# Attention and a four-expert layer on one core: second products only in runs of two token tiles

## The chip, the core and the metric

The kernel runs on one core of a Trainium2 chip. The metric is the device time of one execution in microseconds (us), the median of several runs; less is better.

## What is computed

The reference is block-sparse attention followed by a mixture of four experts, all in float32.

```python
# attention: batch 4, 8 heads, 768 tokens, head size 64, blocks of 32 tokens
scores = q @ k.T / 8
mask = |block_i - block_j| <= 1, or first/last block on either side, or one of 3 sampled blocks
attn = softmax(where(mask, scores, -1e9)); x = (attn @ v) as [3072 tokens, 512]
# experts: 512 -> 1024 -> 512, weighted by normalised probabilities p
for e in range(4):
    out += p[:, e:e+1] * (maximum(x @ w1[e], 0) @ w2[e])
```

## The kernel before

TensorE (PE in the rows) does nearly all of the work, on float32 values split into a high and a low part (`copy` to fp32r and a subtraction), so that one product is three matmuls.

The tokens come in five sets: batch 0 as two plain sets of 384 tokens, batches 1 to 3 as sets of 768. Each set runs through eight chunks of 512 hidden columns (four experts, two chunks each).

- A **first product** (`first`, L714) makes one piece of the hidden layer: six matmuls of 384 columns into one bank of PSUM, `w` or `v`. The plain sets take eight a chunk (`PLAIN`, two per hidden tile; L725 in the rows). The last three sets use a Strassen-like scheme with seven products of half size for eight; a chunk is two halves of `2, 1, 5, 6, 3, 7, 4` (`ORDER`, L628; L746). Products 2, 5 and 3 go to bank `v`, the others accumulate in bank `w`, which product 1 opens anew. Readers take intermediate sums out of the banks: ScalarE copies `v` after 2 (L767) and 5 (L773); VectorE adds out of `w` after 1 (L769), 6 (L776) and 7 (L781), and out of `v` after 3 (L778). A finished hidden tile gets ReLU on ScalarE (`hh`, L753; in the plain sets L734) and its low part on VectorE (`hl`, L754; L735). The last tile of a half is read straight out of `w`: after product 4, `hh` and then `hl` must be done before the next half's product 1 may write `w`.
- A **second product** (`second`, L787) multiplies one hidden tile (index f, 0 to 3) of one token tile (j, 0 to 2) with `w2`: three matmuls of 512 columns (L795) into one of three banks `po`, one for each token tile. After f = 3 VectorE adds the bank into the output rows `oacc` (L810); the next round may then write the bank.

Operands are made seven first products ahead (`operands`, `NWO`): ScalarE casts (L674), GpSimd subtracts (L675), and VectorE makes the sums of weights in place (L678 to L684; L682 overwrites what L675 read). `split_w2` (L692) does the same for `w2` (L698, L699).

Attention for the next batch (units `Group` and `Edge`) is fed in between: scores into two banks (`S`, L347 and L480), transposes into the same two banks (`T`, L385 and L502), weighted values (`A`, L416 and L531). Gathered rows come by GpSimd's DMA (L212). `attend` (L1008) places each part by a count of product time; the scores are placed only after a second product (`drive(..., 2)`). At the end of a batch `conversion` (L582) turns the attention output into the seven operands of the next set; VectorE does large subtractions there (L597, L594), starting eight first products before the set ends.

The order of products is fixed when the program is built, in `experts` (L827): `lead` gives each second product the count of first products after which it is due, ten or more after its tile was begun. A step yields either one second product, if due, or one first product. `hl` of a first product is recorded one step later (`defer`), behind whatever that step records on VectorE.

Of the kernel before, what the change touches and what calls it, by code (L numbers as in the profile page):

```python
# [23 lines left out]
def attention_moe_kernel(ctx: ExitStack, tc, qb, kb, vr, sampled, sampled_t, probs, w1, w2, out):  # L24
# [193 lines left out]
    one = const.tile([1, 1], F32, name="one")  # L218
# [8 lines left out]
    lead = p1.tile([NR, G], F32, name="lead")  # L227
# [392 lines left out]
    def convert(b, r):  # L620
        if b in todo and todo[b][0][0] <= r:
            step(b)

    def need(b, n):
        while b in todo and any(m == n for _, _, m in todo[b]):
            step(b)
# [5 lines left out]
    def plain(m):  # L632
        return m < 2
# [80 lines left out]
    def first(b, c, s, n):  # L714
        ps_m, cp, hp = later["m"], later["c"], later["h"]
        w = wo.pop((b, c, s, n))
        if plain(b):
# [10 lines left out]
            if k == 1:  # L728
                f = 2 * s + i
                ring = int((c * FT + f + FT) % (NH[0] + NH[1]) >= NH[0])  # L730
                hh = hp.tile([P, HS], F32R, name=f"hh{ring}", bufs=NH[ring])
                hl = hp.tile([P, HS], F32R, name=f"hl{ring}", bufs=NH[ring])
                src = W[s]
# [16 lines left out]
        def finish(half, g, src):  # L750
            hh = hp.tile([P, HS], F32R, name=f"hh{g}", bufs=NH[g])
            hl = hp.tile([P, HS], F32R, name=f"hl{g}", bufs=NH[g])
            nc.scalar.activation(hh, src, AF.Relu)  # L753
            defer.append(lambda: nc.vector.scalar_tensor_tensor(hl, src, 0.0, f32(hh), op0=ALU.max,  # L754
                                                                op1=ALU.subtract))
            hs[c, 2 * s + half, g] = (hh, hl)
# [65 lines left out]
    TB = NCH * (len(ORDER) * T1 + KT * FT * T2)  # L822
    TP = NCH * (len(PLAIN) * T1 + KT // 2 * FT * T2)
    OFF = 10
    NH = (5, 3)

    def experts():  # L827

        sets = []
        ends = [0]  # L830
        for b in range(SETS):
            sets.append(([(b, c, s, n) for c in range(NCH) for s, n in (PLAIN if plain(b) else ORDER)],
                         [(b, c, g, f, j) for c in range(NCH) for g in ((0,) if plain(b) else (1, 0))
                          for f in range(FT) for j in range(HS // P)]))
            ends.append(ends[-1] + len(sets[-1][0]))
        one = [x for a, _ in sets for x in a]
        two = [x for _, a in sets for x in a]

        lead = [ends[b] + i * len(a) / len(t) + OFF for b, (a, t) in enumerate(sets) for i in range(len(t))]

        def ready(p):

            q = 0
            for b, (a, t) in enumerate(sets):
                q += min(max(p - OFF + 1 - ends[b], 0), len(a)) * len(t) // len(a)
            return q

        p = q = 0
        after_first = False
        while q < len(two):  # L850

            left = defer[:]
            defer.clear()
            wait = after_first and p < len(one) and one[p][3] == 4 and q < ready(p)
            if wait or p >= min(len(one), lead[q]):
                second(*two[q])
                q += 1
                after_first = False
                took = T2, 2
            else:  # L860
                need(one[p][0], one[p][3])
                first(*one[p])
                p += 1
                after_first = True
                took = T1, 1
            for op in left:
                op()
            for b in todo:
                if p - ends[b] >= EARLY:
                    convert(b, p - ends[b])  # L870
                    break
            yield took

    stream = experts()
    done = [0.0]

# [238 lines left out]
```

## Time and profile before

| | us |
|---|---|
| median of 3 runs | 1249.38 (1248.95 to 1249.69) |
| profiled execution | 1256.33 |
| its span | 1254.6 |
| TensorE matmuls busy | 1228.3 |
| VectorE / ScalarE / GpSimd busy | 759.5 / 675.6 / 715.1 |

The profiled execution is one run, taken with the profiler on; its own time stands beside the span that the rows cover. Matmuls overlap, so the length of a row is longer than the time until the next one starts; the distance of two starts is what a piece costs TensorE. Some rows merge several matmuls.

### The profile page before, as it was taken

How to read it: one execution, taken by the hardware profiler on the slowest of the kernel's cores; microseconds unless marked ns; L12 is line 12 of the kernel's file. 1: busy time of each engine (PE TensorE's matmuls, PEld its weight loads, DVE VectorE, ACT ScalarE, POOL GpSimd, SP SyncE). 2: the span in 40 equal slices, each digit the busy share in tenths (PEclk: the TensorE clock that was granted, in tenths of full speed). 3: DMA queues.
4: the chain of work that ended last, by engine and by line, in shares of the span. 5: the costliest groups of instructions: out<-in, count | busy, mean ns of one | idle time of the engine just before them, and what ended most of it. 6: DMA issues, size and time to landing. Idle time of an engine off the chain costs nothing.

```text
span 1254.6 us, 29430 instructions
## 1 busy us (share of the span) xinstructions
PE 1228.3 (98%) x11028; PEld 1051.0 (84%) x11028; DVE 759.5 (61%) x1743; ACT 675.6 (54%) x1817; POOL 715.1 (57%) x846
## 2 busy tenths in 40 slices
PE   5899999999999999999999999999999999999998
PEld 3688888878888888888888888888888888888887
DVE  5455536545448676656658676666756855555553
ACT  4556645666656446666665445666664544444441
POOL 5566656666659646555546664556544855555551
PEclk9899999999999999999999999999999999999999
DMA  8556646585635425444413442444431222222211
GB/s 242 159 184 172 192 167 214 181 233 183 189 104 196 152 77 153 151 126 124 131 60 131 160 125 84 138 153 135 142 91 47 89 97 66 67 70 68 66 51 54
DMA packets 75051, 163.84 MB, mean 131 GB/s; under 512 B 8923, under 2 KB 20188, under 8 KB 74908
## 3 DMA queue, kind: packets, MB, share of 16 engines
q1 hardware_dynamic: 69238, 144.65, 36.8%
q0 software_dynamic: 5632, 17.31, 5.0%
q8 instruction: 87, 1.43, 0.5%
q14 instruction: 56, 0.46, 0.1%
q10 hardware_dynamic: 38, 0.00, 0.0%
HBM read 155.63 MB, written 6.29 MB: 129 GB/s over the span
## 4 chain that ended last, share of the span: by engine, by line
PE 67%; DVE 2%; issue 0%; POOL 0%; POOLq 0%; DVEq 0%
PE po L795 32%; PE w L746 16%; PE v L746 12%; PE s L347 2%; PE o L416 2%; PE tp L385 1%; DVE oacc L810 1%; PE ow L531 1%; PE sw L480 1%; PE tw L502 0%; DVE d L597 0%; DVE hl L754 0%; DVE r L682 0%; PE w L725 0%; PE v L725 0%
## 5 line engine op out<-in xcount | busy, mean ns | idle before, releaser
L675 POOL TENSOR_TENSOR wo<-r,wo 128x256 fp32r<-128x256 f32 x288 | 241.2, 840 | 278.5 <-ACT wo L674 275.0
L795 PE MATMUL po<-h,hh 128*128 128x512 f32 x768 | 307.4, 400 | 1.4 <-DVE oacc L810 1.4
L795 PE MATMUL po<-h,hl 128*128 128x512 f32 x768 | 304.5, 397 | 0.0
L795 PE MATMUL po<-l,hh 128*128 128x512 f32 x768 | 303.5, 395 | 0.1
L746 PE MATMUL w<-xo,wo 128*128 128x384 f32 x1152 | 233.2, 337 | 0.2 <-DVE u L776 0.2
L699 POOL TENSOR_TENSOR l<-r,h 128x512 fp32r<-128x512 f32 x160 | 211.2, 1320 | 37.6 <-ACT h L698 36.9
L746 PEld LDWEIGHTS w<-xo,wo 128*128 128x128 f32 x1152 | 205.4, 188 | 19.2 <-DVE z L781 0.8
L746 PE MATMUL v<-xo,wo 128*128 128x384 f32 x864 | 176.1, 338 | 0.0
L795 PEld LDWEIGHTS po<-h,hl 128*128 128x128 f32 x768 | 143.8, 187 | 31.6 <-issue 0.3
L746 PEld LDWEIGHTS v<-xo,wo 128*128 128x128 f32 x864 | 154.6, 188 | 13.0 <-ACT z L773 0.2
L661 POOL TENSOR_TENSOR wo<-r,wo 128x256 fp32r<-128x256 f32 x128 | 95.8, 750 | 116.4 <-ACT wo L660 109.2
L795 PEld LDWEIGHTS po<-h,hh 128*128 128x128 f32 x768 | 144.2, 188 | 20.4 <-DVE oacc L810 2.8
L795 PEld LDWEIGHTS po<-l,hh 128*128 128x128 f32 x768 | 144.2, 188 | 12.4
L674 ACT CAST wo<-r 128x256 fp32r<-128x256 f32 x288 | 114.3, 397 | 49.1 <-PE w L746 31.3
L810 DVE SCALAR_TENSOR_TENSOR oacc<-po,pr,oacc 128x512 f32<-128x512 f32 x168 | 124.1, 741 | 24.1 <-PE po L795 24.0
L374 ACT ACTIVATE p<-p,mx 128x256 f32<-128x256 f32 (+1 forms) x192 | 95.4, 498 | 69.6 <-DVE mx L371 69.6
L698 ACT CAST h<-r 128x512 fp32r<-128x512 f32 x160 | 99.0, 619 | 11.5 <-PE po L795 11.3
L212 POOL DMA_INDIRECT v<-in_vr_dram,vidx x88 | 85.1, 967 | 26.6 <-issue 18.4
L371 DVE CUSTOM_DVE_ANT_1 p<-s,mask 128x256 f32<-128x256 f32 (+1 forms) x192 | 69.8, 418 | 49.1 <-PE s L347 38.6
L725 PE MATMUL w<-xo,wo 128*128 128x384 f32 x384 | 80.5, 342 | 1.1 <-issue 1.0
L725 PE MATMUL v<-xo,wo 128*128 128x384 f32 x384 | 78.4, 340 | 0.5 <-ACT xo L322 0.5
L769 DVE TENSOR_TENSOR p<-w,p 128x384 f32<-128x384 f32 x48 | 26.7, 555 | 84.8 <-PE w L746 81.6
(148 smaller groups left out, 1666.7 us busy)
## 6 DMA issues: line engine op xcount, KB each, us to landing
r<-in_w_dram SPq DMA_DIRECT2D x80, 512.0 KB
r<-in_w_dram SPq DMA_DIRECT2D x160, 256.0 KB
v<-in_vr_dram SPq DMA_DIRECT2D x44, 384.0 KB
kr<-in_kb_dram SPq DMA_DIRECT2D x76, 192.0 KB
k<-in_kb_dram SPq DMA_DIRECT2D x8, 768.0 KB
v<-in_vr_dram SPq DMA_DIRECT2D x12, 512.0 KB
out_dram<-oacc SPq DMA_DIRECT2D x23, 256.0 KB
q<-in_qb_dram SPq DMA_DIRECT2D x20, 256.0 KB
```

Of the source, the lines that this page charges most:

```text
L212: nc.gpsimd.indirect_dma_start(out=v[:G, i, 1], out_offset=None, in_=vr, element_offset=b * S * DM, in_offset=bass.IndirectOffsetOnAxis(ap ...
L371: nc.vector.tensor_tensor_reduce(p.rearrange("p (a b) -> p a b", b=BLOCK), s[h][:n, i], mk, -SCALE, 3.0e38, ALU.add, ALU.min, mx[:n])
L374: nc.scalar.activation(p, p, AF.Exp, bias=mx[:n], scale=-1.0, accum_out=self.sums[:n, m:m + 1])
L661: nc.gpsimd.tensor_sub(o[:, 1], r[s][:, i, k], f32(o[:, 0]))
L674: nc.scalar.copy(o[:, 0], src)
L675: nc.gpsimd.tensor_sub(o[:, 1], src, f32(o[:, 0]))
L698: nc.scalar.copy(h, r)
L699: nc.gpsimd.tensor_sub(l, r, f32(h))
L725: nc.tensor.matmul(W[s], w[:, wi, t], x[xi][:, k * KH + t], start=k == 0 and m == 0, stop=k == 1 and m == 3 * KH - 1)
L746: nc.tensor.matmul(ps, w[:, wi, t], x[:, xi, t], start=fresh and m == 0, stop=m == 3 * KH - 1, skip_group_check=not fresh)
L795: nc.tensor.matmul(p, a[:, js], w, start=f == 0 and n == 0, stop=f == FT - 1 and n == 2)
L810: nc.vector.scalar_tensor_tensor(accs[tok], p, pe, accs[tok], op0=ALU.mult, op1=ALU.add)
```

## The change

The rule that picks the next step. Before, a second product went out as soon as it was due. Now second products go out only when two are due (or when all that remain are), and then both in a row. In front of product 4, if a first product was just made, up to two ready ones are taken early. Until two are due, first products go on.

```diff
@@ attention_moe_kernel @@
     OFF = 10
+    RUN = 2
     NH = (5, 3)
@@ experts @@
-        p = q = 0
+        p = q = burst = 0
         after_first = False
         while q < len(two):
...
-            wait = after_first and p < len(one) and one[p][3] == 4 and q < ready(p)
-            if wait or p >= min(len(one), lead[q]):
+            if not burst:
+                due = sum(1 for n in range(q, min(q + RUN, len(two))) if p >= min(len(one), lead[n]))
+                if due == min(RUN, len(two) - q):
+                    burst = due
+                elif after_first and p < len(one) and one[p][3] == 4:
+                    burst = min(RUN, ready(p) - q)
+            if burst:
+                burst -= 1
                 second(*two[q])
                 q += 1
                 after_first = False
```

What this does to the order, at three places.

On TensorE, in the last set, from product 4 of one half (on `w`) to product 1 of the next. Before:

```order
L746 MATMUL w<-xo_14346,wo 128x384 x6
L795 MATMUL po<-h_16029,hh_16110 128x512
L795 MATMUL po<-l_16030,hh_16110 128x512
L795 MATMUL po<-h_16029,hl_16111 128x512
L746 MATMUL v<-xo_14180,wo 128x384 x6
L795 MATMUL po<-h_16029,hh_16110 128x512
L795 MATMUL po<-l_16030,hh_16110 128x512
L795 MATMUL po<-h_16029,hl_16111 128x512
L795 MATMUL po<-h_16029,hh_16110 128x512
L795 MATMUL po<-l_16030,hh_16110 128x512
L795 MATMUL po<-h_16029,hl_16111 128x512
L746 MATMUL w<-xo_14205,wo 128x384 x6
```

and now:

```order
L746 MATMUL w<-xo_14347,wo 128x384 x6
L746 MATMUL v<-xo_14171,wo 128x384 x6
L795 MATMUL po<-h_16044,hh_16110 128x512
L795 MATMUL po<-l_16045,hh_16110 128x512
L795 MATMUL po<-h_16044,hl_16111 128x512
L795 MATMUL po<-h_16044,hh_16110 128x512
L795 MATMUL po<-l_16045,hh_16110 128x512
L795 MATMUL po<-h_16044,hl_16111 128x512
L746 MATMUL w<-xo_14201,wo 128x384 x6
```

One second product stood between 4 and 2; now 2 follows 4 at once, and between 4 and 1 stand two seconds where there were three.

On VectorE, at the first conversion (end of the plain sets). The three L810 add the three token tiles of one round into the output; L597 are the conversion's subtractions. Before:

```order
L810 SCALAR_TENSOR_TENSOR oacc<-po,pr,oacc 128x512
L597 TENSOR_TENSOR d_6342<-xr 128x768
L597 TENSOR_TENSOR xr<-xr,d_6342 128x2x384
L810 SCALAR_TENSOR_TENSOR oacc<-po,pr,oacc 128x512
L678 TENSOR_TENSOR s_6377<-r_6246 128x256
L597 TENSOR_TENSOR d_6343<-xr 128x768
L810 SCALAR_TENSOR_TENSOR oacc<-po,pr,oacc 128x512
L735 SCALAR_TENSOR_TENSOR hl_6375<-v,hh_6374 128x384
```

and now:

```order
L810 SCALAR_TENSOR_TENSOR oacc<-po,pr,oacc 128x512
L597 TENSOR_TENSOR d_6342<-xr 128x768
L597 TENSOR_TENSOR xr<-xr,d_6342 128x2x384
L678 TENSOR_TENSOR s_6373<-r_6246 128x256
L597 TENSOR_TENSOR d_6343<-xr 128x768
L810 SCALAR_TENSOR_TENSOR oacc<-po,pr,oacc 128x512
L735 SCALAR_TENSOR_TENSOR hl_6371<-v,hh_6370 128x384
L810 SCALAR_TENSOR_TENSOR oacc<-po,pr,oacc 128x512
```

The second tile's L810 stood ahead of L678 and the third subtraction; now it is behind them.

On VectorE, at the second conversion. `hl_10238` is the low part after product 4, which frees bank `w`; L678 belongs to product 2's operand work. Before:

```order
L781 TENSOR_TENSOR z_10142<-w,z_10142 128x384
L597 TENSOR_TENSOR d_10156<-xr 128x768
L754 SCALAR_TENSOR_TENSOR hl_10212<-z_10142,hh_10211 128x384
L597 TENSOR_TENSOR xr<-xr,d_10156 128x2x384
L754 SCALAR_TENSOR_TENSOR hl_10238<-w,hh_10237 128x384
L678 TENSOR_TENSOR s_10260<-r_10067 128x256
L597 TENSOR_TENSOR d_10157<-xr 128x768
```

and now:

```order
L781 TENSOR_TENSOR z_10138<-w,z_10138 128x384
L597 TENSOR_TENSOR d_10164<-xr 128x768
L754 SCALAR_TENSOR_TENSOR hl_10212<-z_10138,hh_10211 128x384
L597 TENSOR_TENSOR xr<-xr,d_10164 128x2x384
L678 TENSOR_TENSOR s_10256<-r_10067 128x256
L754 SCALAR_TENSOR_TENSOR hl_10238<-w,hh_10237 128x384
L597 TENSOR_TENSOR d_10165<-xr 128x768
```

L678 has moved ahead of that `hl`. The two products' order explains it: `hl` is recorded one step after its product, and that step is now product 2.

## Rows read from the trace of the kernel before

**Rows 1.** The page: the engine table (busy us, share of the span, instructions), and the granted TensorE clock in 40 slices of the span, in tenths of full speed.

```profile
PE 1228.3 (98%) x11028; PEld 1051.0 (84%) x11028; DVE 759.5 (61%) x1743; ACT 675.6 (54%) x1817; POOL 715.1 (57%) x846
PEclk9899999999999999999999999999999999999999
```

**Rows 2.** Busy time by stage: start:end in us, length, then busy us and instructions of TensorE's matmuls, its weight loads, VectorE, ScalarE and GpSimd, then the granted clock, the DMA share and GB/s.

```profile
372.00:1000.00 628.00, 626.46 (x5503) 536.68 (x5502) 434.34 (x932) 361.60 (x963) 365.92 (x413) 1.00 0.40 123
1000.00:1243.00 243.00, 243.00 (x1208) 218.06 (x1207) 129.87 (x228) 95.79 (x224) 123.61 (x133) 1.00 0.21 64
```

**Rows 3.** The timeline of TensorE in the stage with products alone: start us, length us, engine, line, operation, output and inputs, number of instructions merged. The rows are single matmuls of seconds (L795) and whole firsts (L746); the last one opens the next half chunk at the same first product.

```profile
1018.69 0.39 PE L795 MATMUL po<-h,hh 128*128 128x512 f32 x1
1019.39 1.22 PE L746 MATMUL v<-xo,wo 128*128 128x384 f32 x6
1020.45 0.39 PE L795 MATMUL po<-h,hh 128*128 128x512 f32 x1
1021.84 1.21 PE L746 MATMUL w<-xo,wo 128*128 128x384 f32 x6
1035.07 1.22 PE L746 MATMUL v<-xo,wo 128*128 128x384 f32 x6
```

**Rows 4.** The timeline of TensorE where firsts stand in a row early on, twelve matmuls to a row, and from the chain that ended last its piece of 16 seconds in a row.

```profile
57.01 2.24 PE L725 MATMUL v<-xo,wo 128*128 128x384 f32 x12
59.09 2.24 PE L725 MATMUL w<-xo,wo 128*128 128x384 f32 x12
1238.46 10.94 PE po L795 x48
```

**Rows 5.** The waits of TensorE's matmuls: total us, times, longest.

```profile
PE po L795 <- DVE oacc L810: 1.4, 3, 0.5
PE w L725 <- issue: 1.0, 4, 0.3
```

**Rows 6.** The timeline of TensorE behind two attention groups: the first matmul of a second and the first that follows it, and a first and the second that follows it.

```profile
485.87 0.50 PE L795 MATMUL po<-h,hh 128*128 128x512 f32 x1
486.67 0.51 PE L746 MATMUL v<-xo,wo 128*128 128x384 f32 x2
500.52 1.34 PE L746 MATMUL v<-xo,wo 128*128 128x384 f32 x6
501.69 0.39 PE L795 MATMUL po<-h,hh 128*128 128x512 f32 x1
```

**Rows 7.** The timeline of TensorE behind another attention group, a first and the second after it. The record merges five of the first's six matmuls.

```profile
277.55 1.52 PE L725 MATMUL w<-xo,wo 128*128 128x384 f32 x5
279.58 0.40 PE L795 MATMUL po<-h,hh 128*128 128x512 f32 x1
```

**Rows 8.** The timelines of GpSimd, VectorE and TensorE around 529 us, in the attention of batch 2; in brackets what ended the idle time before.

```profile
525.22 0.92 POOL L212 DMA_INDIRECT v<-in_vr_dram,vidx  x1 [0.30 <-issue]
526.16 1.30 POOL L699 TENSOR_TENSOR l<-r,h 128x512 fp32r<-128x512 f32 x1
527.41 0.74 POOL L675 TENSOR_TENSOR wo<-r,wo 128x256 fp32r<-128x256 f32 x1
528.19 2.19 DVE L682 TENSOR_TENSOR r<-s,r 128x256 f32<-128x256 f32 x1 [2.28 <-POOL wo L675]
531.10 0.50 PE L795 MATMUL po<-h,hh 128*128 128x512 f32 x1 [0.47 <-DVE oacc L810]
```

**Rows 9.** The timelines of VectorE and TensorE at the first conversion.

```profile
374.38 1.61 DVE L597 TENSOR_TENSOR d<-xr 128x768 f32<-128x768 f32 x1
376.02 1.37 DVE L597 TENSOR_TENSOR xr<-xr,d 128x768 f32<-128x768 f32 x1
378.32 2.05 DVE L597 TENSOR_TENSOR d<-xr 128x768 f32<-128x768 f32 x1
380.30 0.74 DVE L810 SCALAR_TENSOR_TENSOR oacc<-po,pr,oacc 128x512 f32<-128x512 f32 x1
373.51 1.21 PE L725 MATMUL v<-xo,wo 128*128 128x384 f32 x6
381.09 0.50 PE L795 MATMUL po<-h,hh 128*128 128x512 f32 x1 [0.41 <-DVE oacc L810]
```

**Rows 10.** The timelines of VectorE and TensorE at the second conversion. The first at 672.24 is 2, that at 674.75 is 1.

```profile
672.18 2.04 DVE L597 TENSOR_TENSOR xr<-xr,d 128x768 f32<-128x768 f32 x1
674.15 0.55 DVE L754 SCALAR_TENSOR_TENSOR hl<-w,hh 128x384 fp32r<-128x384 f32 x1
674.62 0.49 DVE L678 TENSOR_TENSOR s<-r 128x256 f32<-128x256 f32 x1
675.03 1.49 DVE L597 TENSOR_TENSOR d<-xr 128x768 f32<-128x768 f32 x1
672.24 1.22 PE L746 MATMUL v<-xo,wo 128*128 128x384 f32 x6
674.75 1.31 PE L746 MATMUL w<-xo,wo 128*128 128x384 f32 x6
```

**Rows 11.** The timelines of VectorE and TensorE at a 4 in the attention of batch 1.

```profile
443.51 0.56 DVE L754 SCALAR_TENSOR_TENSOR hl<-w,hh 128x384 fp32r<-128x384 f32 x1 [1.50 <-ACT hh L753]
442.10 1.22 PE L746 MATMUL v<-xo,wo 128*128 128x384 f32 x6
444.55 1.21 PE L746 MATMUL w<-xo,wo 128*128 128x384 f32 x6
```

## The prediction

> **What bounds the kernel now.** I read the page's engine table first, then busy time by stage, TensorE's timeline, and the waits. The table has TensorE busy for 1228.3 us of a span of 1254.6, with the granted clock at its upper level (2.4 GHz) in all but the first slices [rows 1]. By stage nothing is left over: 626.46 of 628 us where attention and products mix, 243.00 of 243 once only products are left [rows 2]. So the time is the sum of TensorE's pieces plus a few short waits. A reordering can only change what a piece costs beside its neighbour, or the waits.
>
> The pieces, from start to next start. With products alone [rows 3], a first product takes 1.06 us (1019.39 to 1020.45), a single second 0.70 (1018.69 to 1019.39), two in a row 1.39 (1020.45 to 1021.84). A half chunk, seven firsts and twelve seconds, takes 15.68 (1019.39 to 1035.07) without a gap. Where firsts stand in a row, two take 2.08 (57.01 to 59.09), 1.04 each, and sixteen seconds in a row 10.94, so 0.68 each [rows 4]. A switch of kind thus costs some hundredths at most.
>
> The waits given to TensorE's matmuls past the start are few: three for an accumulation (1.4 us), four that nothing in the profile ends (1.0 us) [rows 5].
>
> **The change, part by part.** Counts are from the built order. Both kernels issue the same 464 firsts, 768 seconds, attention groups, casts and transfers; nothing is added. Single seconds between two firsts go from 121 to none. A half chunk of the last three sets was 2 ss 1 ss 5 ss 6 s 3 ss 7 ss 4 s (s a second); now each of the seven but one has ss behind it, and 4 and the next 2 stand in a row. In the plain sets one pair of firsts in every four does.
>
> (a) Switches. Before 7 x 1.045 + 2 x 0.698 + 5 x 1.389 = 15.66 us a half chunk, now 6 x 1.045 + 1.040 + 6 x 1.389 = 15.64 (third digits: medians of the starts behind [rows 3, 4]). 12 ns saved in 46 halves and 32 plain groups of four is **-0.9 us**. Bounds: 0, and -2.6 if all of 15.68 - 7 x 1.04 - 12 x 0.68 = 0.24 us lies evenly on 14 switches, of which two go. I take the smaller, as single and paired seconds have rows of their own.
> The Trainium skill (TensorE: Matmul & The Clock Gate, Back-to-back issue gap) gives a spacing by the column count alone, N/2.4 GHz plus 2.5 ns. By that no order of the same matmuls is cheaper: (a) is zero and the sum 0.9 us higher. Its 0.65 us for three matmuls of 512 columns is under every row here, so I do not follow it.
>
> (b) Attention's neighbours. A group lengthens a first behind it to 1.17 (500.52 to 501.69), a second to 0.80 (485.87 to 486.67) [rows 6]: 0.12 and 0.10. Groups followed by a first go from 42 to 33, by a second from 79 to 88; seconds before a group from 87 to 91, which I price alike. -9 x 0.12 + 9 x 0.10 + 4 x 0.10 is **+0.2 us**, bounds +-0.9.
>
> (c) Gaps that nothing ends. Behind two dense groups a first took 2.03 us (277.55 to 279.58) [rows 7], and so at two more places within 50 us. All three followed attention directly with a first; where a second followed, none occurred. At two of the three a second stands there now. I take half of the gain, **-0.8 us**, as the cause has no row; bounds -2.6 and +2.6 (all go; three more).
>
> (d) Late subtractions in attention. At 531.10 TensorE was some 0.6 us late for a bank (0.47 of it idle in the record). GpSimd's operand (L675, 527.41) stood behind a gather and L699, VectorE's L682 ran from 528.19 for 2.19, and the accumulation L810 was behind that [rows 8]. The same again 299 us later. In the new order L699 (1.30) follows that L675, so L682 can start sooner; but the accumulations of two tiles, not one, now stand behind L682, and the first is wanted 2.4 us after its matmuls in place of 3.5. Both weighed: **-0.4 us**, bounds -1.3 and +2.2.
>
> (e) The first conversion. VectorE runs d 1.61, xr 1.37 and a second d 2.05 us, and at 381.09 TensorE was 0.6 us late (0.41 of it idle in the record) for the third tile's accumulation, begun at 380.30 [rows 9]. In the new order the second tile's accumulation stands behind all three too, since its product now follows two firsts. From the rows: the firsts start at 373.51 and 374.55, two seconds at 375.6, a first at 377.0, two seconds at 378.0; the second of these, at 378.7, needs that accumulation, which ends when 376.02 + 1.37 + 0.35 + 2.0 + 0.7 = 380.4 is reached. A wait of 1.7 in place of 0.6: **+1.1 us**, bounds -0.6 and +2.
>
> (f) The release of bank w at the two later conversions. First 1 overwrites w and so waits for hl of the 4 before. In between stood s 2 ss, now 2 ss: 0.70 less. There a 2.04 us subtraction (L597) is ahead of that hl on VectorE; hl began at 674.15, and 1 at 674.75, 0.06 late [rows 10]. In the new order L678 (0.41 to the next start) moves ahead of hl too. From these rows: 2 starts at 672.24 - 0.70 = 671.54, the two seconds at 672.58, and 1 could at 673.97; but L597 ends at 674.2, hl at 675.1, so 1 starts near 675.16, a wait of 1.2 in place of 0.06. Two places: **+2.3 us**. Bounds: 0 (L597 at the 1.49 of its other row, later waits absorbed) and +4 (VectorE stays behind for the next 4).
>
> (g) The same release where ScalarE is late. hl 443.51 to 444.07, with 2 started at 442.10 [rows 11]; in the new order 2 would start 0.70 sooner and 1 at 441.40 + 1.04 + 1.39 = 443.83, 0.3 too early. With its twin 299 us later **+0.5 us**, bounds 0 and +1.5.
>
> Covered: the reads of w behind 1, 6 and 7 and of v behind 5 keep a first and two seconds, or two seconds, before the next write, no less than before; operands are made seven firsts ahead.
>
> Sum: -0.9 + 0.2 - 0.8 - 0.4 + 1.1 + 2.3 + 0.5 = +2.0 us. The profiled execution lasted 1256.33 us (span 1254.6 and 1.7 around it), 7 over the median of three runs; the change is added to that median, 1249.38: **1251.4 us**. A measurement here can tell about 0.2%, 2.5 us, from no change.
>
> **The rivals.**
> 1. *VectorE releases w too late in many halves* (slower). TensorE has 2.4 us of work between 4 and 1 where it had 3.1; it decides where hl ends over 2.3 us after 4. For it: (f), and that L678 is now ahead of every such hl. Against: without attention VectorE is busy 129.87 of 243 us [rows 2], with room. If ten of the 30 halves with attention pay 0.4, and (e) and (f) their upper ends (+2.6 more): 1251.4 + 6.6 - (g) 0.5 = 1257.5; half of it 1254.5.
> 2. *The old waits go and none takes their place* (faster). (c), (d) and (e) at their lower ends, -4.5, (a) -0.9, (f) and (g) 0: 1244.0; with half of (c) 1245.3. Against: L597 and L678 stand ahead of hl whatever the timing.
> 3. *Two firsts in a row outrun their operands* (slower). An operand costs GpSimd 0.74 us [rows 8], two firsts take 2.08 of TensorE; decides where the seven ready ones run out. If 46 pairs paid 0.1: 1256. Against: seconds still space the firsts 2.2 us apart on the mean.
> 4. *The change does little*, since attention still cuts pairs: 1249.4.
>
> **How the numbers follow.** Forecast 0.62, rival 1 0.17, rival 2 0.13, rival 3 0.03, rival 4 0.05. The forecast's own spread, some +-2 us from (c), (e) and (f), lies across the bound at +2.5: 0.40 of its 0.62 under it, 0.22 over. Same 0.40 + 0.05 = 0.45, slower 0.22 + 0.17 + 0.03 = 0.42, faster 0.13. The range takes the forecast with its bounds and the near halves of rivals 1 and 2: 1247.2 to 1255.4.
>
> **What would show it.** In the changed profile: half chunks without attention of 15.64 to 15.68 us; no single seconds of 0.70 between firsts; a first on w waiting about 1 us behind hl at both later conversions, a second waiting over 1 us on L810 at the first; fewer gaps behind attention. A wait on hl in most halves, waits on L675, or a half chunk off 15.6 to 15.7 would prove it wrong.

## The result: 12 us slower

| | before | after |
|---|---|---|
| median of 6 runs each, us | 1249.54 | 1261.49 |
| lowest and highest | 1248.55 to 1250.85 | 1260.03 to 1264.33 |
| ratio | 1 | 1.0096 [1.0086, 1.0107] |
| profiled execution (span) | 1256.33 (1254.6) | 1260.18 (1258.5) |

The forecast was 1251.4 with a range to 1255.4; the time lies above all of it. The medians differ by 12.0 us, the two profiled executions by 3.9 only. A second profile of the kernel before, among the experiments, tells why, and it is the one that the sums below go by.

The page after: the engine table's line of TensorE and the others, and the granted clock.

```profile
PE 1219.9 (97%) x11028; PEld 1047.1 (83%) x11028; DVE 768.8 (61%) x1743; ACT 677.2 (54%) x1817; POOL 702.3 (56%) x846
PEclk9999999999999999999999999999999999999999
```

Against [rows 1] TensorE is busy 8.4 us less, with the clock at 90% or more of full speed in every slice. Busy time by stage, columns as in [rows 2]:

```profile
372.00:1000.00 628.00, 615.57 (x5450) 526.48 (x5450) 423.55 (x921) 355.94 (x950) 348.43 (x406) 1.00 0.39 120
1000.00:1243.00 243.00, 242.30 (x1208) 217.64 (x1208) 140.63 (x231) 97.11 (x227) 122.61 (x135) 1.00 0.21 66
```

Where attention and products mix, 12.4 us of 628 are now without a matmul; there were 1.5. The 0.7 us that the other stage lost is the end of the third conversion's last wait, just past 1000. Inside its half chunks nothing is lost, as TensorE's timeline there shows (4, 2, and the 4 of the next half):

```profile
1178.55 1.20 PE L746 MATMUL w<-xo,wo 128*128 128x384 f32 x6
1179.60 1.20 PE L746 MATMUL v<-xo,wo 128*128 128x384 f32 x6
1194.19 1.20 PE L746 MATMUL w<-xo,wo 128*128 128x384 f32 x6
```

From 4 to the next half's 4 is 15.64 us (1178.55 to 1194.19) where [rows 3] had 15.68, and 4 to 2 is 1.05. The pairs do there what the forecast said. The loss stands in the waits of TensorE's matmuls (total us, times, longest), which answer to [rows 5]:

```profile
PE po L795 <- DVE oacc L810: 6.8, 8, 2.1
PE w L746 <- DVE z L781: 4.6, 2, 2.3
PE w L746 <- DVE hl L754: 3.0, 2, 1.5
```

Nearly all of it is in the three conversions. The first one, VectorE's timeline and then TensorE's; the answer to [rows 9]:

```profile
366.28 1.61 DVE L597 TENSOR_TENSOR d<-xr 128x768 f32<-128x768 f32 x1
367.93 1.38 DVE L597 TENSOR_TENSOR xr<-xr,d 128x768 f32<-128x768 f32 x1
369.23 0.96 DVE L678 TENSOR_TENSOR s<-r 128x256 f32<-128x256 f32 x1
370.11 2.03 DVE L597 TENSOR_TENSOR d<-xr 128x768 f32<-128x768 f32 x1
372.07 0.74 DVE L810 SCALAR_TENSOR_TENSOR oacc<-po,pr,oacc 128x512 f32<-128x512 f32 x1
369.93 0.39 PE L795 MATMUL po<-h,hh 128*128 128x512 f32 x1
372.86 0.51 PE L795 MATMUL po<-h,hh 128*128 128x512 f32 x1 [2.07 <-DVE oacc L810]
```

The second tile's accumulation (372.07) stands behind the last of three large subtractions, and the second product that needs its bank starts at 372.86 in place of about 370.6. Some 20 us later the same tile is late again, now behind a low part (L594):

```profile
388.88 1.49 DVE L594 TENSOR_TENSOR xo<-d,xo 128x768 fp32r<-128x768 f32 x1
390.29 0.74 DVE L810 SCALAR_TENSOR_TENSOR oacc<-po,pr,oacc 128x512 f32<-128x512 f32 x1
388.97 0.39 PE L795 MATMUL po<-h,hh 128*128 128x512 f32 x1
391.09 0.50 PE L795 MATMUL po<-h,hh 128*128 128x512 f32 x1 [1.26 <-DVE oacc L810]
```

The second conversion, bank `w` after product 4, the answer to [rows 10]:

```profile
667.86 2.05 DVE L597 TENSOR_TENSOR xr<-xr,d 128x768 f32<-128x768 f32 x1
669.83 0.94 DVE L678 TENSOR_TENSOR s<-r 128x256 f32<-128x256 f32 x1
670.69 0.54 DVE L754 SCALAR_TENSOR_TENSOR hl<-w,hh 128x384 fp32r<-128x384 f32 x1
668.96 0.39 PE L795 MATMUL po<-h,hh 128*128 128x512 f32 x1
671.29 1.31 PE L746 MATMUL w<-xo,wo 128*128 128x384 f32 x6 [1.48 <-DVE hl L754]
```

The low part (670.69) waits out the subtraction of 2.05 us and L678, and product 1 starts at 671.29, 1.65 late. Then, 15 us further on, comes a wait that the forecast had under "covered": product 4 for the addition out of `w` behind product 7.

```profile
685.02 0.96 DVE L594 TENSOR_TENSOR xo<-xr,xo 128x768 fp32r<-128x768 f32 x1 [0.47 <-ACT xo L590]
685.89 0.55 DVE L781 TENSOR_TENSOR z<-w,z 128x384 f32<-128x384 f32 x1
683.36 0.39 PE L795 MATMUL po<-h,hh 128*128 128x512 f32 x1
686.50 1.32 PE L746 MATMUL w<-xo,wo 128*128 128x384 f32 x6 [2.29 <-DVE z L781]
```

The addition (L781, 685.89) takes 0.55 us, but it stands behind the low part of operand 6, which itself had waited for ScalarE's high part. Product 4 is 2.45 us late. In the kernel before, the same addition stood ahead of that low part, and product 4 began 0.05 us after it:

```profile
685.86 0.55 DVE L781 TENSOR_TENSOR z<-w,z 128x384 f32<-128x384 f32 x1
686.33 1.02 DVE L594 TENSOR_TENSOR xo<-xr,xo 128x768 fp32r<-128x768 f32 x1
686.46 1.31 PE L746 MATMUL w<-xo,wo 128*128 128x384 f32 x6
```

To add such waits up I took each piece of TensorE's work and the median of the pieces of its kind between the same kinds of neighbours in the first profile of before; what is longer by over 0.12 us counts as late. At the conversions that gives 5.6 us at the first (2.23, 1.42, 0.40, 1.59), 5.3 at the second (1.65, 0.37, 2.45, 0.85) and 5.4 at the third (the same places): **16.4 us**. In the second profile of before it is 0.84.

### The profile page after: what moved, and what is told of

The parts are those of the page before. It is cut to its first block, busy times and chain, and to the rows that moved or that the text cites. A ratio compares the mean times of both kernels' runs of the same rounds, so it can differ in the third digit from the quotient of the medians.

```text
span 1258.5 us, 29422 instructions
## 1 busy us (share of the span) xinstructions
PE 1219.9 (97%) x11028; PEld 1047.1 (83%) x11028; DVE 768.8 (61%) x1743; ACT 677.2 (54%) x1817; POOL 702.3 (56%) x846
## 4 chain that ended last, share of the span: by engine, by line
PE 89%; DVE 6%; issue 2%; ACT 1%; POOL 0%; DVEq 0%; ACTq 0%; POOLq 0%
PE po L795 40%; PE w L746 15%; PE v L746 11%; PE w L725 5%; PE v L725 5%; PE s L347 3%; PE o L416 3%; PE tp L385 3%; PE ow L531 1%; PE sw L480 1%; DVE xo L594 1%; DVE oacc L810 1%; PE tw L502 1%; DVE hl L754 1%; DVE xr L597 1%
## 5 line engine op out<-in xcount | busy, mean ns | idle before, releaser
L675 POOL TENSOR_TENSOR wo<-r,wo 128x256 fp32r<-128x256 f32 x288 | 233.8, 816 | 311.4 <-ACT wo L674 310.9
L795 PE MATMUL po<-h,hh 128*128 128x512 f32 x768 | 308.6, 402 | 6.8 <-DVE oacc L810 6.8
L795 PE MATMUL po<-h,hl 128*128 128x512 f32 x768 | 304.5, 396 | 0.0
L795 PE MATMUL po<-l,hh 128*128 128x512 f32 x768 | 303.2, 395 | 0.0
L746 PE MATMUL w<-xo,wo 128*128 128x384 f32 x1152 | 232.9, 336 | 7.6 <-DVE z L781 4.6
L746 PEld LDWEIGHTS w<-xo,wo 128*128 128x128 f32 x1152 | 205.3, 188 | 25.9 <-DVE z L781 5.5
L746 PE MATMUL v<-xo,wo 128*128 128x384 f32 x864 | 174.5, 336 | 0.0
L795 PEld LDWEIGHTS po<-h,hh 128*128 128x128 f32 x768 | 144.2, 188 | 31.4 <-DVE oacc L810 9.9
L795 PEld LDWEIGHTS po<-h,hl 128*128 128x128 f32 x768 | 143.9, 187 | 31.2
L746 PEld LDWEIGHTS v<-xo,wo 128*128 128x128 f32 x864 | 153.4, 188 | 8.5
L795 PEld LDWEIGHTS po<-l,hh 128*128 128x128 f32 x768 | 144.2, 188 | 15.0
L661 POOL TENSOR_TENSOR wo<-r,wo 128x256 fp32r<-128x256 f32 x128 | 95.0, 745 | 94.8 <-ACT wo L660 87.9
L810 DVE SCALAR_TENSOR_TENSOR oacc<-po,pr,oacc 128x512 f32<-128x512 f32 x168 | 122.1, 741 | 32.0 <-PE po L795 31.6
L698 ACT CAST h<-r 128x512 fp32r<-128x512 f32 x160 | 98.8, 617 | 15.6 <-PE po L795 15.3
L398 ACT ACTIVATE p<-p,rec 128x256 f32<-128x256 f32 (+1 forms) x132 | 63.0, 505 | 27.7 <-DVE rec L406 27.5
```

The costliest lines, as they stand in the source:

```text
L661: nc.gpsimd.tensor_sub(o[:, 1], r[s][:, i, k], f32(o[:, 0]))
L675: nc.gpsimd.tensor_sub(o[:, 1], src, f32(o[:, 0]))
L698: nc.scalar.copy(h, r)
L746: nc.tensor.matmul(ps, w[:, wi, t], x[:, xi, t], start=fresh and m == 0, stop=m == 3 * KH - 1, skip_group_check=not fresh)
L795: nc.tensor.matmul(p, a[:, js], w, start=f == 0 and n == 0, stop=f == FT - 1 and n == 2)
L810: nc.vector.scalar_tensor_tensor(accs[tok], p, pe, accs[tok], op0=ALU.mult, op1=ALU.add)
```

## The experiments

Differences in us are the ratio's, or those of the medians of one comparison; all were timed beside the kernel before on the same chip. The chips differ: the kernel before took 1249.4 to 1250.3 us in most comparisons and 1255.8 to 1255.9 in two (those without the large subtractions or the low parts, and single ones at the later two). There the differences to before are to be read, not the times.

### Is it the conversions, and is it the pairs there?

**Single second products at the conversions, pairs elsewhere.** Two lines of the rule:

```diff
+                run = RUN if not any(-10 <= p - e <= 10 for e in ends[2:SETS]) else 1
-                due = sum(1 for n in range(q, min(q + RUN, len(two))) if p >= min(len(one), lead[n]))
-                if due == min(RUN, len(two) - q):
+                due = sum(1 for n in range(q, min(q + run, len(two))) if p >= min(len(one), lead[n]))
+                if due == min(run, len(two) - q):
...
-                    burst = min(RUN, ready(p) - q)
+                    burst = max(0, min(run, ready(p) - q))
```

> The rule of before (one second as soon as it is due) from ten first products before to ten after the end of the second, third and fourth set; pairs everywhere else. Theory A (the loss is made at the three conversions, where VectorE's queue is the limit; waits there grew from 1.2 to 16.4 us): those waits go back to about 1 us and the rest keeps its small gain, 1244 to 1248 us, under the 1249.5 of before. Theory B (the loss is spread over attention's stages): 1258 to 1261 us.

Measured: 1245.20 us beside 1249.36, ratio 0.9967 [0.9955, 0.9979]. That is 4.2 us *under* the kernel before; the waits past the start are down to

```profile
PE po L795 <- DVE oacc L810: 0.4, 1, 0.4
PE w L746 <- DVE u L776: 0.4, 2, 0.2
```

So all of the loss, and more, is at the conversions; pairs elsewhere are worth 4 us.

**The reverse: pairs at the conversions alone.**

The edit, against the run above:

```diff
-                run = RUN if not any(-10 <= p - e <= 10 for e in ends[2:SETS]) else 1
+                run = RUN if any(-10 <= p - e <= 10 for e in ends[2:SETS]) else 1
```

> The reverse: pairs only from ten first products before to ten after those three set ends, the rule of before everywhere else. Theory A: nearly all of the conversions' 15 us is paid without the gain elsewhere, 1262 to 1266 us. Theory B: 1250 to 1253 us.

Measured: 1254.71, ratio 1.0040 [1.0027, 1.0054], 5.3 over, which neither theory had. Its conversions' waits are 7.6 us, not 16.4. In the built order the pairs differ by one: here tiles pair as (2, next round's 0) at a round's end and product 4 has two seconds behind it, in the changed kernel they pair as (1, 2) and 4 has none. Which second is the first of a pair therefore decides as well.

**The same alignment everywhere.**

```diff
+            if q == 0 and burst:
+                burst = 1
             if burst:
                 burst -= 1
```

> The changed kernel, but the very first second product goes out alone, so every later pair begins one second product later in the list: a round of twelve ends with its last tile paired with the next round's first. Second products still go only in pairs, at the conversions too. Theory A1 (the alignment of the pairs to the rounds decides which products stand together and how long an accumulation has): as in the run with pairs only at the conversions, some 7 to 8 us of waits at the conversions in place of 16, 1251 to 1254 us. Theory A2 (pairs as such cost the 16 us at the conversions): 1260 to 1263.

Measured: 1256.59 beside 1249.93, ratio 1.0055 [1.0041, 1.0069]; 6.7 over, so 5 better than the change but outside both expectations. The conversions' waits are 6.9 us, as the first theory had it. What it missed are 6 us of waits in the attention of the second plain set, the largest of 2.9 us behind a VectorE operation; the rows are in the last section. The alignment's part is shown in size, not why this one fits the conversions better in each place.

**Single ones at the later two only** (`ends[3:SETS]` in the first edit).

> Pairs everywhere, single second products within ten first products of the second and third conversion alone; the first conversion is as in the changed kernel. If the cost adds up by place, as the waits in the changed kernel's profile do (5.6 us at the first conversion, 5.3 at each of the others): 5 us over the run with single ones at all three, 1249.5 to 1251. If the first conversion's waits do not reach the end: 1245 to 1246.5. If most of the cost is there: 1255 or more.

Measured: ratio 1.0019 [1.0010, 1.0028] to the kernel before, 0.52% over the run with single ones at all three, so 6.5 us (its time, 1258.30, stands beside 1255.92). The first conversion's waits are 7.2 us in this profile, 0.6 with single ones. The cost adds up by place, somewhat more than expected; 1.6 us of the 7.2 are a first and two seconds that ran at the lower clock behind a wait (last section).

### Which operations make the waits?

**Place of one low part, and of the low parts `hl`.** Two small edits: operand 6's low part one step later; and the deferred `hl` recorded ahead of a first product's own operations.

```diff
-                   (-2, hi(6, b12), 0), (-2, None, 0), (-2, lo(6, b12, nc.vector), 6),
+                   (-2, hi(6, b12), 0), (-2, None, 0), (-1, None, 0), (-1, lo(6, b12, nc.vector), 6),
```

> The changed kernel, with the conversion's third low part (VectorE L594 of operand 6) recorded one step later, so that VectorE's add behind product 7 (L781) stands ahead of it as it did before the change. If the place in VectorE's queue makes the 2.45 us wait of product 4 on L781, those two waits go: about 1256.5 us (5 us less). If VectorE is merely too full there, the wait turns up later: 1260 to 1262 us.

```diff
                 need(one[p][0], one[p][3])
+                for op in left:
+                    op()
+                left = []
                 first(*one[p])
```

> The changed kernel, with the low part hl of a product recorded ahead of the next step's own work when that step is a first product, so that hl behind product 4 stands ahead of L678 again. The step of the prediction (f): the wait of product 1 at the second and third conversion shrinks from 1.65 by L678's 0.9 us to 0.7, so about 1259.5 us. If L678's place does not matter: 1261.5 us, with the wait unchanged.

Measured: 1260.62 (ratio 1.0089 [1.0074, 1.0105]) and 1261.90 (1.0103 [1.0087, 1.0118]). Neither helps. In the first the wait of 2.45 us at the addition falls to 1.0, and 1.7 come back at the next half's product 1 (691.35): its `hl` now stands behind the moved low part (687.05), the fourth subtraction (L597, 688.47) and L678 (689.88). The low part delays whatever stands behind it. In the second the waits on `hl` do fall from 1.65 to 0.78 us at both later conversions, as (f) has it, and the 1.59 at the first conversion is gone. But at the second conversion the wait at product 4 is now followed by slower matmuls (last section), and a wait of 1.99 us for an accumulation has come up at 830 us, in the attention.

**The large subtractions sooner**, with the change, and with single seconds at the conversions:

```diff
-    EARLY = -8
+    EARLY = -13
...
-        todo[b] = [(EARLY, less(d5, b12, b11), 0), (EARLY + 1, less(b12, b22, d5), 0),
-                   (EARLY + 2, less(d7, b12, b11), 0),
+        todo[b] = [(EARLY, less(d5, b12, b11), 0), (EARLY + 2, less(b12, b22, d5), 0),
+                   (EARLY + 4, less(d7, b12, b11), 0),
```

> The changed kernel, with the conversions' three large subtractions (L597) due at 13, 11 and 9 first products before the set ends in place of 8, 7 and 6. In the built order all three then stand ahead of the reads of product 3 at the two later conversions, none of them ahead of the low part after product 4; the first conversion hardly changes, since its input is not ready sooner. Theory A (each wait belongs to one large operation that stands ahead of a short one which TensorE wants): the wait of 1.65 us on hl at each of the later two goes, the 2.45 at the z addition and the first conversion's 5.6 stay, 1257.5 to 1258.5 us. Theory C (VectorE is full for some 30 us and carries a backlog from wait to wait): the later waits at the same conversions shrink as well, 1253 to 1256. Neither: 1261.5.

> Pairs everywhere but within ten first products of a conversion (as in the run with single ones there), and the three large subtractions due at 13, 11 and 9 first products before the set ends. In that run the conversions' waits were 2.2 us in all; the later two can lose up to 0.6 each. Theories A and C: 1243.8 to 1245.4 us. If the earlier subtractions only move a wait into the attention's end, 1246 to 1248.

Measured: 1259.73 (ratio 1.0081 [1.0067, 1.0095]) and 1245.10 (0.9965 [0.9951, 0.9979]). With the change both waits of 1.65 us on `hl` are gone, as theory A had it. But behind the wait at the second conversion's product 4 the granted clock fell to its lower level for the next pieces: from product 4 to the next half's product 1 it is 5.15 us (684.57 to 689.72), 3.60 in the changed kernel. The gain, 1.9 us by the ratios, is short of A in the median and far from C; the two of the five executions with the highest granted clock took 1257.2 and 1257.7 us, where A had them. With single seconds it makes no difference to the run without it.

**The large subtractions left out**, from the change and from the kernel before (`None` in place of the four `less`; 5 and 7 read `b11` and `b12`).

> The changed kernel without the four large subtractions (L597) of each conversion; products 5 and 7 then take their operands from quarters that exist already, and 3, 4 and 6 take theirs unsubtracted, so the output is another one. All other work, the four low parts (L594) on VectorE among it, is as in the changed kernel. Theory A (each wait belongs to the one large operation ahead): only the waits directly behind L597 go, 2.2 us at the first conversion and 1.65 at each later one, 1255.5 to 1257. Theory C (VectorE is full for some 25 us at a conversion, and what it is late by at one wait it is still late by at the next): nearly all 16 us of waits go, 1245 to 1247.5.

> The kernel before without the same four subtractions: what they cost there. Its second profile had 0.6 us of waits at the first conversion and 0.4 us at the two others. Theories A and C: 1248 to 1249.4 us, no difference that can be told. If the subtractions slow more than the waits show (GpSimd's operations run beside them), 1245 to 1247.

Measured: 7.3 us over the kernel before (1263.26 beside 1255.92, ratio 1.0062 [1.0047, 1.0076]), and 1.3 under (0.9991 [0.9982, 1.0000]). The waits directly behind L597 are gone, the two of 2.43 us and the 1.45 and 1.59 at the first conversion stand. Theory C falls: VectorE does not carry its lateness through. Under A the low parts must make the rest.

**The low parts given to GpSimd** (`nc.gpsimd` for operands 1, 5, 6 and 7; the first of four such lines is shown), with the change, with the earlier subtractions too, and with single seconds:

```diff
-                   (-4, hi(1, b11), 0), (-4, lo(1, b11, nc.vector), 1),
+                   (-4, hi(1, b11), 0), (-4, lo(1, b11, nc.gpsimd), 1),
```

> The changed kernel, with the four low parts of a conversion that VectorE makes (L594, for products 1, 5, 6 and 7) made by GpSimd. Theory A (each wait at a conversion belongs to one large VectorE operation ahead of a short one): the waits behind low parts go, 2.43 and 0.85 us at each later conversion and about 2 us at the first, the ones behind L597 stay; 3 to 5 us over the kernel before in place of 12. Rival: GpSimd is then late with the weights' low parts (L675) and TensorE waits for operands, 8 us over before or more.

> The same, and the large subtractions due at 13, 11 and 9 first products before the set ends. Theory A: nothing large then stands ahead of a short operation at the later two conversions and the first one's 2.2 us and what follows it is left: 2 us under the kernel before to 2 over. If VectorE's and GpSimd's operations delay each other whatever their order, 5 to 8 over.

> Pairs but for single second products within ten first products of all three conversions, and the low parts made by GpSimd. With single ones the waits at the conversions were 2 us in all, so there is little left to take away: 4 to 5.5 us under the kernel before, as with single ones alone. If GpSimd is late with L675 there: 0 to 3 under.

Measured: 1263.90, 1257.43 and 1259.36 beside 1250.27; ratios 1.0112 [1.0096, 1.0127], 1.0062 [1.0048, 1.0076] and 1.0073 [1.0059, 1.0087]. The first is over by more than its rival's 8 us, but TensorE waits there for accumulations and not for operands; the second lies in its rival's 5 to 8; the third is outside both expectations. It settles that the move itself costs: 9 over before, where single seconds alone are 4 under. GpSimd, VectorE and TensorE there:

```profile
690.79 1.83 POOL L594 TENSOR_TENSOR xo<-d,xo 128x768 fp32r<-128x768 f32 x1
692.59 0.73 POOL L675 TENSOR_TENSOR wo<-r,wo 128x256 fp32r<-128x256 f32 x1
693.35 2.01 DVE L682 TENSOR_TENSOR r<-s,r 128x256 f32<-128x256 f32 x1 [2.46 <-POOL wo L675]
695.28 0.74 DVE L810 SCALAR_TENSOR_TENSOR oacc<-po,pr,oacc 128x512 f32<-128x512 f32 x1
696.08 0.51 PE L795 MATMUL po<-h,hh 128*128 128x512 f32 x1 [2.79 <-DVE oacc L810]
```

GpSimd's weight operand (L675, 692.59) stands behind a low part of 1.83 us, VectorE's L682 waits 2.46 us for it, the accumulation is behind L682, and TensorE stands for 2.79. GpSimd's lateness comes back by VectorE's queue. So these runs could not tell what the low parts cost.

**The low parts left out**, given to no engine; the matmuls read the high part in their place (the first of four such lines is shown):

```diff
-                   (-4, hi(1, b11), 0), (-4, lo(1, b11, nc.vector), 1),
+                   (-4, hi(1, b11), 0), (-4, None, 1),
...
-                    nc.tensor.matmul(ps, w[:, wi, t], x[:, xi, t], start=fresh and m == 0,
+                    nc.tensor.matmul(ps, w[:, wi, t], x[:, xi if n in (2, 3, 4) else 0, t], start=fresh and m == 0,
```

> The changed kernel without the four low parts that VectorE makes at each conversion (L594, for products 1, 5, 6 and 7); the matmuls that would read them read the high part instead, so TensorE does the same work and the output is another one. Nothing is given to another engine. Theory A (each wait belongs to one large VectorE operation ahead of a short one): the waits behind low parts go, 2.4 and 0.9 us at each later conversion and about 2 at the first, those behind L597 stay; 2 to 4.5 us over the kernel before in place of 12. Rival (the waits come from VectorE's order alone, or from GpSimd): 8 to 12 over.

> The changed kernel without the low parts and without the four large subtractions of each conversion. If these eight operations make the whole loss: as with single seconds at the conversions, 3 to 5 us under the kernel before; with the one late L682 after the first conversion left (1.6 us), 2 under. If something else at the conversions takes part: 0 to 6 over.

> The kernel before without the same eight operations, for what they cost there: its conversions have 0.8 to 1.2 us of waits in all. 0 to 2 us under the kernel before.

Measured beside 1255.84: 1259.45 (ratio 1.0027 [1.0016, 1.0038]), 1252.47 (0.9973 [0.9964, 0.9983]) and 1253.54 (0.9983 [0.9974, 0.9992]); 3.6 over, 3.4 under, 2.3 under. The first hits. The second lies in the 3 to 5 under that stood for the whole loss, although the late L682, for which 2 under was expected, is still there; its interval, 2.1 to 4.5 us under, takes in both. The last is just past its edge. Without the low parts TensorE's waits at the conversions are

```profile
PE po L795 <- DVE oacc L810: 3.5, 2, 2.1
PE w L746 <- DVE hl L754: 3.0, 2, 1.5
```

one on `hl` of 1.5 us at each later conversion, and two on accumulations at the first. Without either only one is left, the L682 that comes late after the first conversion:

```profile
PE po L795 <- DVE oacc L810: 1.4, 1, 1.4
```

This is the account. With the pairs the eight operations of each conversion cost 1.0096 - 0.9973 = 1.23%, 15.4 us, the two ratios being from different chips. In the trace, of the 16.4 us of waits 14.5 go; what stays is that L682, 1.59 us late at the first conversion, and two waits of 0.15. Leaving out the large subtractions alone takes away 0.34%, the low parts alone 0.69%. The other 0.2% is no more than the intervals of the four ratios together (0.23%), so it is not shown that a part goes only with both. In the order before, the same operations cost 0.17%, 2.1 us.

What no run separates is how much of the 14.5 us comes from the place of these operations in VectorE's order, and how much from operations there that lasted longer than before, as L678 did: 0.49 us in [rows 10], 0.94 at 669.83 in the changed kernel.

### What the first profile of before did not say

**The kernel before, profiled again.**

> The kernel before, profiled a second time. If its first profile had a start some 4 us longer than usual and three gaps that belong to that execution alone, the first first product begins near 48 us in place of 52.6, the three gaps of 0.75 to 0.95 us behind attention in the plain sets are fewer, and the time is near 1249.5 to 1251 in place of 1256.3. If both belong to the order, the profile is as before.

Measured: 1248.42. The first first product starts at 48.04 us, not at 52.6, and no gap behind attention (as in [rows 7]) is there:

```profile
48.04 1.26 PE L725 MATMUL v<-xo,wo 128*128 128x384 f32 x5 [0.46 <-ACT xo L322]
PE po L795 <- DVE oacc L810: 1.3, 3, 0.5
```

From that start to the last matmul it takes 1194.8 us, the changed kernel 1206.7: 11.9 us, close to the 12.0 of the medians. Both the longer start and the gaps came back in the profile of the kernel before without the large subtractions (50.9 us; gaps of 0.65, 0.80 and 0.91), taken where before itself took 1255.9, and in all six profiles from the two chips on which before took 1255.8 to 1255.9: starts of 49.4 to 52.3 us and three gaps each, with pairs as well as without. The twelve other profiles taken after the first of before start at 47.5 to 49.0 and have one such gap between them. So they go with the chip a kernel was run on, not with the order. Why chips differ is open, and so is on which chip the first profile of before was taken.

## Why the prediction was wrong

What bounds the kernel was read rightly: TensorE's pieces and a few waits. By the terms of the sum, with the second profile of before:

- **(a), (b), pieces.** Forecast -0.7 together. TensorE's pieces without what is late went from 1191.3 to 1188.9 us: -2.4, near the lower bound of (a); the first products alone gave 2.9 (493.0 to 490.0). The half chunk is 15.64, as forecast.
- **(c), gaps behind attention.** Forecast -0.8; nothing to gain, since the gaps went with the chip of the first profile and not with the order. It said that the cause had no row; then the term should have stood in the range, not in the sum.
- **(d), late subtractions in attention.** Forecast -0.4. The waits of 0.64 us at 523.6 and 822.8 us are gone: -1.3, at its better end.
- **(e), the first wait at the first conversion.** Forecast 1.7 in place of 0.6; it was 2.23. The mechanism and the rows were right, the size 0.5 short, since L678 ahead of the third subtraction took 0.96 us (0.88 to the next start) and was priced at 0.35.
- **(f), the release of bank w.** Forecast 1.2 at each of two; it was 1.65, by the mechanism named; here too L678 was the longer one, 0.86 us to the next start where 0.41 was priced.
- **(g).** Forecast +0.5; no such wait over 0.12 us.
- **What failed is the step that (e) and (f) end at the first wait, with the sentence on what is "covered".** It counted TensorE's pieces between a read and the next write and found no fewer. It did not look at where VectorE's other large operations had moved to on that engine. After the two priced places the conversions hold another 10.9 us (16.4 - 2.23 - 2 x 1.65): the additions behind 7 (2.45 and 2.47), the second tile's accumulation in later rounds (1.42, 1.59, 0.85, 0.86) and smaller ones. (f)'s upper bound, VectorE "behind for the next 4", had the right kind at the wrong size: +4 for all that follows two conversions.

So the conversions took 15.6 us more (16.4 - 0.84) where (e) and (f) had 3.4. That the whole is off by 10 us and not by 12 is luck: the terms beside them came out 2.3 us better than forecast (pieces by 1.7, (d) by 0.9, (g) by 0.5, against 0.8 of (c)).

Rival 1 had the engine right, VectorE, but put the late release of bank `w` into the attention's halves; the waits on `hl` came twice, at the two later conversions alone. Of rival 2's old waits those of (d) went, that of (e) grew, and new ones came. Rivals 3 and 4 had no part: TensorE's waits name no weights, and the change did much.

The deeper error is in reading slack. In [rows 10] the first on `w` was 0.06 us late behind VectorE, and at 381.09 [rows 9] a second 0.6: the conversions already ran with nothing to spare. Busy time at the second conversion in the first profile of before, columns as in [rows 2]:

```profile
672.00:692.00 20.00, 20.00 (x99) 17.54 (x98) 18.95 (x25) 12.09 (x25) 17.91 (x14) 1.00 0.47 158
```

VectorE was busy 18.95 of 20 us, with TensorE at 20.00. Here a second engine was 95% busy and TensorE still never stopped: the order happened to fit, and a shift of it has to be followed to the stage's end.

The best version here keeps pairs and goes back to single seconds within ten first products of a conversion: 1245.20, ratio 0.9967 [0.9955, 0.9979], 16 us under the change.

## What to carry to other kernels

A new order is priced where the second-busiest engine is nearly full, and there through the whole stage: list what that engine does in the new order, and ask of each short operation that releases a bank which long one now stands ahead of it. A rule that helps in the steady state can be switched off in the few microseconds where it hurts. And a second profile of the kernel before tells which of its waits belong to the order and which to one execution.

## What the runs showed of the hardware

**VectorE beside GpSimd.** The same subtraction of 128x768 took 0.94 us in one place and 2.56 in another. In the kernel before (first fence), and in the changed one with GpSimd's operation beside it:

```profile
681.67 0.94 DVE L594 TENSOR_TENSOR xo<-xr,xo 128x768 fp32r<-128x768 f32 x1
```

```profile
676.82 2.56 DVE L594 TENSOR_TENSOR xo<-xr,xo 128x768 fp32r<-128x768 f32 x1 [0.30 <-ACT xo L590]
676.71 1.86 POOL L594 TENSOR_TENSOR xo<-xr,xo 128x768 fp32r<-128x768 f32 x1
```

Over the profiles most of VectorE's 128x768 operations stood near 0.95, 1.49, 2.05 and 2.55 us, in steps of about 0.55, with some between; the longest lay inside GpSimd's own subtractions, but some of 0.94 did too. The Trainium skill (SBUF — State Buffer, SBUF: two separate sides) says that a VectorE operation with two SBUF inputs and a GpSimd operation that reads SBUF take a shared port pair in turn, whole instructions at a time. The steps and the longest rows would fit such turns, those of 0.94 us inside a subtraction of GpSimd's only if GpSimd's row counts its own wait. The trace does not show that, nor which of the two began first, so the rows do not settle it. Either way a shift of the order changes VectorE's durations as well.

The longest such row is in the run with pairs shifted by one. GpSimd, VectorE (two operations in the row), TensorE, and busy time of TensorE, its weight loads, VectorE, ScalarE and GpSimd, then the granted clock:

```profile
266.60 0.92 POOL L212 DMA_INDIRECT v<-in_vr_dram,vidx  x1 [0.31 <-DMA kr<-in_kb_dram]
267.54 1.30 POOL L699 TENSOR_TENSOR l<-r,h 128x512 fp32r<-128x512 f32 x1
268.79 1.41 POOL L661 TENSOR_TENSOR wo<-r,wo 128x256 fp32r<-128x256 f32 x2
270.15 1.26 POOL L699 TENSOR_TENSOR l<-r,h 128x512 fp32r<-128x512 f32 x1
267.05 4.78 DVE L400 TENSOR_SCALAR p<-p,rec 128x256 f32<-128x256 f32 x2
271.72 1.39 PE L385 MATMUL tp<-ident,p 128*128 128x128 f32 x8 [2.88 <-DVE p L400]
272.00:276.00 4.00, 4.00 (x18) 3.71 (x16) 0.30 (x1) 1.17 (x2) 0.00 (x0) 0.57 0.58 186
```

With GpSimd busy without a break from 266.60 to 271.41, two operations of VectorE lasted 4.78 us. In the run with single seconds the same two took

```profile
265.57 2.19 DVE L400 TENSOR_SCALAR p<-p,rec 128x256 f32<-128x256 f32 x2
```

There GpSimd was busy too, but only until 267.61. In both runs the two operations ended just after GpSimd's unbroken work did: 271.83 after 271.41, and 267.76 after 267.61. That fits VectorE being held up by GpSimd; no run takes GpSimd's work away to show it.

**TensorE's clock behind a wait.** In the run with pairs shifted by one TensorE then stood for 2.88 us, and from 272 to 276 its granted clock was 0.57 on the mean, so mostly at the lower level (1.2 GHz). So that wait cost its own length and the slower matmuls behind it. In the profile of the changed kernel, with TensorE idle for up to 2.31 us at a time, the granted clock was 1.00 in every stretch of 8 or 10 us at the three conversions. The length of a wait alone does not tell the two apart. With the large subtractions sooner, the wait at the second conversion's product 4 was followed by the lower level (TensorE's rows, then busy time with the granted clock as above):

```profile
684.57 1.49 PE L746 MATMUL w<-xo,wo 128*128 128x384 f32 x6 [2.27 <-DVE z L781]
685.86 2.12 PE L746 MATMUL v<-xo,wo 128*128 128x384 f32 x6
686.00:688.00 2.00, 2.00 (x8) 2.00 (x7) 1.19 (x2) 1.52 (x3) 1.18 (x2) 0.50 0.00 0
```

Product 2 (685.86) took 1.92 us to the next start where it took 1.05 in the changed kernel (687.66 to 688.71). At the third conversion of the same run, behind the same 2.27 us, the clock was 1.00 from 984 to 992. It was 0.50 behind the same wait at the second conversion in the run with `hl` recorded sooner (686 to 689) and in the one without the large subtractions (689 to 692), and behind 2.06 us at the first conversion with single ones at the later two (380 to 383). Executions of one kernel differ with it: with the large subtractions sooner, 1257.22 and 1257.65 us at a mean granted clock of 0.997 and 0.998, 1259.73 to 1260.70 at 0.993 to 0.995. Why one wait is followed by the lower level and another of the same length is not, these runs do not show.
